# Segment handoff of a recurrent attention kernel: the turned output projection in PSUM, its swap on ScalarE and VectorE, and a new instruction order

## The chip, the cores and the metric

The kernel runs on one core of a Trainium2 chip. The metric is the device time of one launch in microseconds (us). Its engines are TensorE (PE in the profile, its weight loads PEld), VectorE (DVE), ScalarE (ACT), GpSimd (POOL) and SyncE (SP), which issues nearly all DMAs. Matmul results land in PSUM, which here is eight banks of 512 fp32 columns on 128 partitions; everything else that engines read lies in SBUF.

## What is computed

Two attention branches over the same 2048 x 512 input are mixed by a gate. Branch A is a recurrence: 64 segments of 32 tokens, each attending to itself and to 8 memory rows, and the memory of the next segment is the attention's own output at the memory rows. So the segments can't run in parallel. Branch B is an attention over four stretches of 512 tokens with a compressive memory, 32 heads of width 16, and doesn't depend on A.

```python
def _A_ref(x, mem0, Wq, Wk, Wv, Wo, seg_len):        # H=32 heads, Dh=128, M=8
    mem = mem0
    for s in range(n_seg):                           # 64
        xs = x[:, s * seg_len:(s + 1) * seg_len, :]  # 32 tokens
        h = jnp.concatenate([mem, xs], axis=1)
        q, k, v = (jnp.einsum('btd,dhe->bhte', h, W) for W in (Wq, Wk, Wv))
        scores = jnp.einsum('bhqe,bhke->bhqk', q, k) * scale
        p = softmax(where(mask, scores, -1e9))
        o = jnp.einsum('bhqk,bhke->bhqe', p, v)
        o = jnp.einsum('bhte,hed->btd', o, Wo)
        mem = o[:, :M, :]
        outs.append(o[:, M:, :])
...
return g * a + (1 - g) * b                           # g: sigmoid gate, b: branch B
```

## The kernel before

**Recorded operations, one fixed order.** Each piece of work is recorded with `P.op(engine, function, reads, writes, cost, prio)` or `P.dma(...)` (class `Prog`). Where `engine` is a tuple, either engine may do it. The order of the operations on each engine, and with it the choice between such engines, is not decided at build time: it is decoded from a packed string `ORDER` by `sequences()`. `schedule()` replays this order to assign PSUM banks, and `waits()` then derives the semaphore waits from the recorded reads and writes. For a PSUM bank, readers on different engines are put one after the other (`_add`, the loop over `r.readers`); readers on the same engine need no wait.

**One segment** (`p_seg`). From `hT`, the transposed input of the segment (24 of its tokens and the 8 memory rows on the columns, in two buffers used in turn), `project` makes keys, queries and values (matmuls in L1413, copies out of PSUM in L1002). `ktr` transposes keys and queries (L1483), `p_s` makes scores (L1498, L1502) and their exponentials (L1506), `p_u` sums (L1521), logarithm and reciprocal (L1525, L1527) and normalises (L1529, L1531), `f_pv` and `f_pw` multiply with the values (L1562, L1571), and L1002 copies the result into `OT`. Then `wo` makes the output projection.

**The handoff** (`wo` with `mem`). The 64 matmuls of L1310 leave, in 256 columns of one PSUM bank (`so`), four partial results on four groups of 32 partitions: two halves of the heads by two halves of the 512 output columns. The next segment needs the 8 memory rows, transposed and summed over the two halves of the heads, in `hT[1 - par][:, :, 24:32]`. Four steps get them there:

- the turn, L1329: VectorE transposes the 256 columns in 32 x 32 blocks into the tile `rc_sb`;
- two swaps, L1332: 64 partitions each change sides, 32 columns, from `rc_sb` to `rc_sb`, on ScalarE or GpSimd;
- the addition, L1334: VectorE adds the 32 turned and the 32 swapped columns of `rc_sb` into `hT`.

The first projection of the next segment waits for that. Beside it, the segment's own rows leave the same bank: a copy of one half to SBUF (`par`, L1336 by way of L1002, on ScalarE or VectorE) and the row addition L1342 into `ao`, from where a DMA takes them to HBM. After that the bank is free.

**Filler.** Between a segment's dependent steps TensorE does work that doesn't hang on the recurrence: keys, queries and values of the remaining 8 tokens of each segment, four segments at a time (`p_rest`, operand `xr` in L1413; their output projection is `wor`, operand `OTr_sb` in L1310), and all of branch B (L1025 and L1027, L1142 logits with the exponentials of L1160 and the masks of L1166 on GpSimd, L1183, and in `p_bout` the multiplications of L1217 on VectorE or GpSimd). Their places in the order decide how much stands between the last output projection and the first matmul that needs the addition.

Of the kernel before, what the change touches and what calls it, by code (L numbers as in the profile page):

```python
# [7 lines left out]
ACT = mybir.ActivationFunctionType  # L8
ALU = mybir.AluOpType
# [10 lines left out]
    "tQ3F7hsUJr(E}cQ2Vff0LY4_Gapld#8q6^|@KasVT?tP>;{8RK8LP&4Tfpi_POsYA9rJKN2Q|&(>I10Z13d9!aaR93HJpkWlA;jb$Gw6sJ3`6YD?Ogu)r;+d;n!J<UJ3N)V)Vpm&"  # L20
    "H0PIL<K934t1hX4DGSVC&irXItS$5jX2`mq0r8><BGOiHSf|gorw~mPz=UnXH^S(sBC_K1<hj}LjAJ;?4`wVfWm$A7V0P0hr;`{Td>SF^Yy+V~g5fz5B1~}(Yr2(A0hT6ynJz(NS"
    "WiTz$a-Thz{Bc?!6Jy;o|l4G<XXj~fF{>SWD)sHwC^j@Ue<o}I>62$bt37U<0JLSu5Vl%2`u<MDd*A=7*&s&1}ov_DOtX5<wU6T<dtX*i0O7xnQYK~5)Ol41o`W8ND%A^QL}dik("
    "^jFEV?v!UY!yBgP$h>#lVh{Tl)Kq-Y|IAN~pTOG17A!V{*gGBH+)bnm7ucR5Ce9{Pq!{!LpBM9meDUSU`Z3N?V*bAep%37Q#%NYte6}jEwb*e*Cmj)XIR)odv5RQdtt&73qRMjO>"
    "&kZW81Q2^ExT(x=+9vtZ|}<p5zGr^H8M%S(av=$rx>wl54Y*>6fdY;wOMO01k%Z*SLAT@7##k}B4h)vjL!kY+Q|IgB~AP#TMpij&Azg*$cck>$!i2J$n^lC>|%y43<Q<D~k~rFFc"
    "N)%-z9^IMK{LqvOHp}Va5L5tsCg%X^Z(`*hn2xC%MaF{@>IEB3hA@~*uSU@hnSEa?o=7I~(brh170C%Uzp*l1JMsET;$GH56N^82&VWCsm;JZ-!$-Ki4VbS65BIVULK|&DJg>Ir^"
    "5cHaKPMRdQHC%T=vo60pkPG=9%w4*BP=5*N#Q@$Fe?k&wbePC;Lc-F{j3aad|CW+q^K9mbtq|3g&PlV=pGrH~HW#y?^VO!mkPjeYY}`m96)gL>Q~<asoTHK6B~<g=rT(dA7tjzL?"
    "t&d3=gU@yvd(?|;S@*HoSp$^2Z;4|I!RF=Y|bQUAO7ccu*lL=#{N7OS|fC>Pnw=3oZ{~+|G>nRCl*><#O32K4l)6Z;76zhDwF33*kb1NB273xorej@p9&c_4;a0N@Elofcf$*_W#"
    "!9Dy@vA7b`x<@MGlfTfw4&ZvI@Fj3-mZXPDvE0PlI71okKH_TkLBN;p6!3x(sB>B#;&Iy@XJdpRD?1zo9#HuEI$Fx)_sV1t-CTAIVJ@2$>*+yHyAYnUI~J1W`N?ei|pdm-*l@&<F"
    "|EfLWKiaT4v0CcI)=G8^_8`pfD!Gy`~Cr5mxFVMt+%<XQc;P<tdakCa7KWyMT@&qCfACY#A-sZ75q%cz;~<M=2wO7BCtI-GZH@N?&aNK}^_fs^zXSz(dsD}^^!;vUC<y+((>$P&;"
    "g-USb)tZ62rZUK3gXO<HBK>=S$_z86UTmmZMJGo$6(QdNVQT|Zl0qhf+2f>dM*znlIY)8ZUHD7vJ!bh!@+KO$!Ld;~Hq>|ipTyKKN4TJ@c$O=nC+3|#s%@X1r0<<Mz_zgNGRD-in"  # L30
    "tgb9AP@CcV(z5>ybGJH2JpgDR!0Z|n{M=qP;R3*D@}?urne%f(LIdQ0drfrNH=2-u?d}WZNpxS!%KZ#39g!xTj!84*>J2$tC(evyvZ-FpAY6dXir?GAR3%-szBmdF2+EU-G8C2Ty"
    "jrGO%KLJT_Z6gW_h)?VwzBpxcGDn$IH8Xk43MrD$Ytwbptr(s0<@~38{l+BS^9!4jU+Q|fVVlOga217Hpj|uN<N3OH=+Jp*_21U2n_%xIYCwl7P)SLV2I-V<7CzfPW2}RDP)-hk9"
    "1`Z9!$}p@FTohC+oWnq+=Z4PZqC#LsV#XOBJ^)!UabgRgqPW8AGDb-CLRB!k*T$=1C<5Th|RpZUrZafdXH84b1Qp1V3CFE9*N*z%u0LFqJ~VlMiKGKvGphmaJYKNZOM`Ql&Vl4h0"
    "kI{pC`VI(b|gAu1$dCx#O?MVZ1pQu`591$ZlK90u*qcRn3Q7*FgIq?h=oN>f0qbI=YTUe-E4djHMn$#IH0l>Dyw%mrJg$tnrc?CNDQh>6kXhOY#Q%Yh7`I&}_Gd|q{qGG0xVXO*1"
    "}qr)tQkRcT)J&fcTAbl+S5DFAbtmb#EPL53&-YB3`EiT>f&@l(@eTFWe^W5_*d6t5bvEYX@fc_SvzUMG<VpMx7E(<UccQ&UZY6GqSskr3YFjxa8A7fNM_XVzZXW*0i2|)=ARQ;1J"
    "0m)P#ydC1y{|n_W;g08Vi1Pt70r&bD$ed~RKjauAq`=<@PCsxR9ts0a4ukG^4DuhpO}r!wQkFOvt^Z-FB;*!I$9k-n|CV7iZTVURoH~<m5t-AM9z#znB3t@5qFlX)M9_lE5WL!qq"
    "Ll0R3gy4~=+_g+mLaTWAr~D*z>ST_l2O4UMJ~8Z@OPkv>Yc^@$#AxrI0l@JACVQpmt!lkKmejky!PCjX?C-LZ^4S&z{M)G&6rfNQUbBrNV=RA7aF{y2$@Di--N}5B$%l>hNm>=FP"
    "IqgQt*z#s}}b>UQVbgqBDghlKRNGV6OF`rVy7Fe~3{qef7sS6!&>OH+ci+@3g1b#Yoh@MKqEsn6{dXQ~t(mGI?dNMr%f)Z2OCH!tDnK=L)R4Vv3PO5vm;RPRz;iljPVNO|XUX$KU"
    "9E@i&oxwZ@<H=uJ_7DHueI!iR_1N&6#IV)HIRGSCqx5nOt5;;;)YqlnFRuI*(P66D;1%M`YjBKd83!4m{`<yQ!-3E?k=H7#x_hJ>`tv9R^70AkDj;oxj@OVCK}Jq8itMPCHTB7W9"
# [12 lines left out]
    "vA;G<rWgIEC1?3y%W{GrBL_*cK(w2%S9|Px)#^}XiXiN5YxMXz#^ENxCg2~CL4`*7UJrGscXW?z7`hDw^w?dJ7MdHx-owfGb%yl7vy$7^uH$8TKpFBLr{0>7};|6Xpw;v8UQzc5e"
    "fL|?x%{hA}aRWJBNja<hDP`si!;N$z`YD--M7_*?vv~$vLfqGu=)adQ%4jdRX6=jhrK_w)W`;SWoM%)SLq^pbF$zfV<!Pa&v;a4`tv+>UTu#<ak)|c`ZziCPh1J6QhGMTW*}(Kn0"
# [1579 lines left out]
```

## Time and profile before

| | us |
|---|---|
| median of 3 runs | 825.1 |
| lowest and highest of them | 824.47 and 826.17 |
| profiled execution | 826.82 |
| its span on the core | 824.9 |

Busy times are sums of an engine's own instructions in that span. A row of a group of instructions has: line, engine, operation, what it writes and reads with its shape, count; then busy us and the mean ns of one; then the idle time of the engine before them, and what ended it. A row of waits has: who waited, for whom, us in total, how often, and the longest. A row of the timeline has start and duration in us. TensorE's matmuls overlap: the record of one is longer than the step to the next, and two tiles of 32 columns run beside each other. The granted clock of TensorE was 0.999 over the span.

### The profile page before, as it was taken

Reading aid. Unit: us, or ns where it says so; the run is one execution under the profiler, and the core shown is the slowest. Engines: PE = TensorE matmul, PEld = TensorE weight load, DVE = VectorE, ACT = ScalarE, POOL = GpSimd, SP = SyncE. Lnnn points to the kernel's source line nnn. Section 1 sums busy time; section 2 is a strip of 40 time slices with the busy share of each in tenths; the row PEclk is TensorE's granted clock in tenths of the full one; section 3 lists DMA queues with packets and bytes.
Section 4 is the critical chain, followed back from the end, with each engine's and each line's share of the span. In section 5 each row is a group of like instructions: output and inputs, shape, how many; then the busy total and the mean of one; then the engine's idle time right before and its main releaser. Section 6 shows DMA issues by size and latency. Waiting matters only on the chain.

```text
span 824.9 us, 51903 instructions
## 1 busy us (share of the span) xinstructions
PE 795.8 (96%) x23652; PEld 500.9 (61%) x23652; DVE 670.5 (81%) x1510; ACT 561.1 (68%) x1306; POOL 269.8 (33%) x627
## 2 busy tenths in 40 slices
PE   9899899999999999999999999999999999999988
PEld 4346576666566566566666666665765665666655
DVE  4789778888779779788888888888877788878887
ACT  3577666777677776667767677687656757766763
POOL 3552322233332333322433322333423224323441
PEclk9999999999999999999999999999999999999999
DMA  8982202121110211111011111100111010010001
GB/s 331 414 242 57 47 17 37 41 52 26 27 45 22 46 26 38 33 39 39 15 39 46 38 27 42 38 14 19 49 37 32 25 38 8 15 25 21 21 21 37
DMA packets 71697, 45.15 MB, mean 55 GB/s; under 512 B 50046, under 2 KB 69942, under 8 KB 69942
## 3 DMA queue, kind: packets, MB, share of 16 engines
q1 hardware_dynamic: 70422, 40.92, 17.3%
q8 instruction: 185, 3.03, 1.6%
q10 hardware_dynamic: 1056, 0.92, 0.4%
q14 instruction: 34, 0.28, 0.1%
HBM read 30.33 MB, written 8.87 MB: 48 GB/s over the span
## 4 chain that ended last, share of the span: by engine, by line
PE 82%; DVE 7%; ACT 4%; DMA 2%; issue 2%; SPq 1%; POOL 1%; ACTq 0%; POOLq 0%; DVEq 0%
PE pb L1413 46%; PE pb L1310 16%; PE pb L1025 6%; PE pb L1142 3%; PE pb L1562 2%; PE pb L1183 2%; DMA Wv_sb<-in_A_Wv_dram 2%; PE pb L1521 2%; PE pb L1498 2%; DVE hT L1334 1%; PE pb L1027 1%; DVE rc_sb L1329 1%; ACT PTB L1160 1%; PE pb L1571 1%; ACT rc_sb L1527 1%
## 5 line engine op out<-in xcount | busy, mean ns | idle before, releaser
L1002 ACT ACTIVATE st<-pb 128x512 bf16<-128x512 f32 (+2 forms) x301 | 143.6, 498 | 81.5 <-PE pb L1413 75.0
L1160 ACT ACTIVATE PTB<-pb 128x640 bf16<-128x640 f32 x240 | 158.9, 703 | 25.9 <-PE pb L1142 19.0
L1413 PE MATMUL pb<-Wv_sb,hT 128*32 128x512 bf16 x2048 | 155.2, 380 | 0.0
L1413 PE MATMUL pb<-Wq_sb,hT 128*32 128x256 bf16 (+1 forms) x3072 | 138.0, 308 | 1.7 <-DVE hT L1334 1.1
L1413 PE MATMUL pb<-Wk_sb,hT 128*32 128x512 bf16 x2048 | 133.9, 380 | 2.8 <-DVE hT L1334 2.2
L1310 PE MATMUL pb<-Wo_sb,OT_sb 128*32 128x256 bf16 x4096 | 130.5, 273 | 2.1 <-issue 1.4
L1310 PEld LDWEIGHTS pb<-Wo_sb,OT_sb 128*32 128x32 bf16 x4096 | 101.2, 96 | 14.6 <-issue 3.8
L1413 PEld LDWEIGHTS pb<-Wq_sb,hT 128*32 128x32 bf16 x3072 | 81.2, 97 | 47.0 <-DVE hT L1334 6.0
L1483 DVE STREAM_TRANSPOSE QT_sb<-st 128x256 bf16<-128x256 bf16 (+1 forms) x192 | 94.0, 507 | 6.1 <-ACT st L1002 4.7
L1166 POOL TENSOR_SCALAR_AFFINE_SELECT PTB<-PTB 128x512 bf16<-128x512 bf16 x120 | 77.4, 645 | 57.8 <-ACT PTB L1160 49.6
L1483 DVE STREAM_TRANSPOSE KT_sb<-st 128x512 bf16<-128x512 bf16 x128 | 89.2, 699 | 8.7 <-ACT st L1002 6.6
L1531 POOL TENSOR_TENSOR PT_sb<-PT_sb,rc_sb 128x64 bf16<-128x64 bf16 x87 | 32.1, 369 | 165.9 <-ACT rc_sb L1527 164.2
L1002 ACT ACTIVATE OT_sb<-pb 128x320 bf16<-128x320 f32 (+1 forms) x138 | 57.3, 427 | 42.4 <-PE pb L1571 42.0
L1413 PEld LDWEIGHTS pb<-Wk_sb,hT 128*32 128x32 bf16 x2048 | 53.4, 96 | 51.5 <-DVE hT L1334 10.5
L1002 DVE CAST OT_sb<-pb 128x320 bf16<-128x320 f32 (+2 forms) x122 | 57.6, 477 | 23.6 <-PE pb L1571 22.4
L1525 ACT ACTIVATE rc_sb<-pb 128x160 f32<-128x160 f32 x128 | 38.8, 303 | 41.6 <-PE pb L1521 38.4
L1002 DVE CAST V_sb<-pb 128x512 bf16<-128x512 f32 x85 | 57.8, 681 | 6.5 <-PE pb L1413 5.1
L1413 PEld LDWEIGHTS pb<-Wv_sb,hT 128*32 128x32 bf16 x2048 | 48.5, 97 | 18.2 <-ACT st L1002 0.6
L1329 DVE STREAM_TRANSPOSE rc_sb<-pb 128x256 f32<-128x256 f32 x63 | 28.2, 448 | 36.4 <-PE pb L1310 36.2
L1506 ACT ACTIVATE PT_sb<-pb 128x224 bf16<-128x224 f32 x128 | 45.4, 354 | 9.4 <-PE pb L1502 7.3
L1529 DVE TENSOR_TENSOR PT_sb<-PT_sb,rc_sb 128x160 bf16<-128x160 bf16 x128 | 43.1, 337 | 6.8 <-ACT rc_sb L1527 5.2
L1413 PE MATMUL pb<-Wv_sb,xr 128*32 128x512 bf16 x512 | 43.6, 381 | 4.3 <-DMA rest_v<-stg 2.2
(202 smaller groups left out, 1458.9 us busy)
## 6 DMA issues: line engine op xcount, KB each, us to landing
Wv_sb<-in_A_Wv_dram SPq DMA_DIRECT2D x4, 1024.0 KB, 9.6
Wk_sb<-in_A_Wk_dram SPq DMA_DIRECT2D x4, 1024.0 KB, 19.9
Wq_sb<-in_A_Wq_dram SPq DMA_DIRECT2D x4, 1024.0 KB, 26.8
Wo_sb<-in_A_Wo_dram SPq DMA_DIRECT2D x4, 1024.0 KB, 22.2
rest_v<-stg SPq DMA_DIRECT2D x112, 32.0 KB
rem_v<-rest_v SPq DMA_DIRECT2D x28, 128.0 KB, 2.5
a_rows<-ao SPq DMA_DIRECT2D x63, 32.0 KB
stg<-a_rows SPq DMA_DIRECT2D x15, 128.0 KB
```

The lines of the kernel that those rows point to most:

```text
L1002: self.P.op(("act", "dve"), (lambda a: a.activation(dst, src(), ACT.Copy), lambda d: d.tensor_copy(dst, src())), reads=reads, writes=write ...
L1025: ins = pe.matmul(out[32 * c:32 * c + 32], lhsT[:, 32 * c:32 * c + 32], rhs, start=start, stop=stop, tile_position=(0, 32 * c), **kw)
L1160: P.op("act", (lambda dst=dst, src=src: lambda a: a.activation(dst, src(), ACT.Exp, scale=0.25))(), reads=[pair], writes=["%s%d_%d" % (nam ...
L1166: P.op("gp", (lambda pt=pt, ii=ii: (lambda g: g.affine_select(pt, pt, ([[0, len(ii)]] if len(ii) > 1 else []) + [[1, 128]], ALU.is_ge, 0.0 ...
L1310: ins = pe.matmul(pb[so.b][p0:p0 + 32, 0:256], tok(r, g, l), half(h, d, q), start=(r == 0 and g == 0 and l < 2), stop=(r == 1 and g == 3 a ...
L1329: P.op("dve", lambda d: d.transpose(rc[:, 0:256], pb[so.b][:, 0:256]), reads=[so], writes=["rc0", "rc1"], name="turn%s" % name, cost=0.45, ...
L1413: ins = pe.matmul(self.pb[sl.b][32 * g:32 * g + 32, 0:hi - lo], x[:, c, 0:32], cols, start=(c == 0), stop=(c == C - 1), tile_position=(0, ...
L1483: op("dve", (lambda dst=dst, src=src: lambda d: d.transpose(dst, src))(), reads=["st%d%s" % (i, tag)], writes=["%sT%d%s" % (kind, r, tag)] ...
L1506: op("act", lambda a: a.activation(PT[:, r, :], pb[rb.b][:, 0:224], ACT.Exp, scale=SCALE), reads=[rb], writes=["PT%d" % r, "PT%dr" % r], n ...
L1525: op("act", lambda a: a.activation(rc[:, r, :], pb[rb.b][:, 0:160], ACT.Ln), reads=[rb], writes=[rr], name="ln%d_%d" % (s, r), cost=t_act( ...
L1529: op("dve", lambda d: d.tensor_tensor(mine[r], mine[r], by_head(rc[:, r, :]), ALU.mult), reads=[rp, rr], writes=[rp], name="nrm%d_%d" % (s ...
L1531: op(("dve", "gp"), tuple((lambda e: e.tensor_tensor(rest[r], rest[r], late(rc[:, r, :]), ALU.mult)) for _ in range(2)), reads=[rp + "r", rr],
```

## The change

The turn writes into the columns 256 to 511 of the same PSUM bank, which were unused. The swaps read there and write a new small SBUF tile `other_sb`; they may stand on ScalarE or VectorE. The addition takes one operand from PSUM and one from `other_sb`. `rc_sb` has no more part in the handoff. Since the swaps and the addition now read the bank, the copy `par`, recorded after them, comes behind them where it is on another engine. The string `ORDER` is new as a whole, so that other operations have moved and changed engines too.

```diff
 ORDER = (
...
+        self.other = t("other_sb", [128, 4, 8], F32)
...
         if mem:
-            rc = self.rc[:, :, :].rearrange("p r x -> p (r x)")
-            turned = rc[:, 0:256].rearrange("p (c e t) -> p e c t", c=4, e=2)
-            other = rc[:, 256:320].rearrange("p (c z) -> p c z", c=4)[:, :, 0:8]
-            P.op("dve", lambda d: d.transpose(rc[:, 0:256], pb[so.b][:, 0:256]), reads=[so], writes=["rc0", "rc1"], name="turn%s" % name, cost=0.45, prio=prio)
+            rt = P.R("turned%s" % name)
+            turned = lambda: pb[so.b][:, 256:512].rearrange("p (c e t) -> p e c t", c=4, e=2)
+            P.op("dve", lambda d: d.transpose(pb[so.b][:, 256:512], pb[so.b][:, 0:256]), reads=[so], writes=[rt], name="turn%s" % name, cost=0.46, prio=prio)
             for e in range(2):
-                dst, src = other[64 * e:64 * e + 64], turned[64 - 64 * e:128 - 64 * e, 1, :, 24:32]
-                P.op(("act", "gp"), ((lambda a, dst=dst, src=src: a.activation(dst, src, ACT.Copy)), (lambda g, dst=dst, src=src: g.tensor_copy(dst, src))),
-                     reads=["rc0", "rc1"], writes=["rcs%d" % e], name="swap%s_%d" % (name, e), cost=(0.24, 0.24), prio=prio)
-            P.op("dve", lambda d: d.tensor_tensor(mem[0], turned[:, 0, :, 24:32], other, ALU.add),
-                 reads=["rc0", "rc1", "rcs0", "rcs1"], writes=[mem[1]], name="hm%s" % name, cost=0.23, prio=prio)
+                dst, src = self.other[64 * e:64 * e + 64], lambda e=e: turned()[64 - 64 * e:128 - 64 * e, 1, :, 24:32]
+                P.op(("act", "dve"), ((lambda a, dst=dst, src=src: a.activation(dst, src(), ACT.Copy)), (lambda d, dst=dst, src=src: d.tensor_copy(dst, src()))),
+                     reads=[so, rt], writes=["other%d" % e], name="swap%s_%d" % (name, e), cost=(0.24, 0.19), prio=prio)
+            P.op("dve", lambda d: d.tensor_tensor(mem[0], turned()[:, 0, :, 24:32], self.other[:, :, :], ALU.add),
+                 reads=[so, rt, "other0", "other1"], writes=[mem[1]], name="hm%s" % name, cost=0.2, prio=prio)
         self.copy(part[64:128, :], lambda: pb[so.b][64:128, 0:256], 256, [so], rhl, "par%s" % name, prio + 0.2 if mem else prio)
```

More of the change, by code (lines that the diff above doesn't have):

```diff
@@ L20 @@
[L20 to L27, printed above, removed]
@@ new lines @@
+    "zC1H3k$WQ((DM{c2-)s&z1LT+tx@?nS6MVx%YTSKUYlS{=Jp=l{0aUCvGZRcUrdSWn;W`iDj}qfD9MXw>P<+q4U3aSkbS3yOLmu(Thk$G!A;%xUhldx<;kj%@;<xw~e#IL#bFV*z"
+    "ob2+?Lf%=xo)4Dw6PJzjf?cm?q3VUR9OAVPK(mX`f}prB6!=bBVao^a0y8R(*#N^Am6a8Dh0*xF@fNy=QJXv)AfPCZ)7$k+C!rC0Gv)z!IYrxlJvbcTAu$RiGyQMY*<PorPrfw^O"
+    "gezet<E%uH2_VU%9_U~LFoOS2Q7l${{yi+E%mz8>(H#Gmoh8bL09WGb8%PMj<WW>`cYrv$8o`E<avLvff;z)t57=>Jq0*Cb>T!<3hBSf@(lq(0q#AKVyzR<c@{if?OWzNFJ=QXqf"
+    "a8f^;#4M+v=g!LJ7MK@d`dS!g<U|iTU61xCm?+AS+FPWdIY7-Sv?oXEPac5E?c>4~dC=>;f1pd$^*!EdW1e3PzT08};GdVT1*pl)nwT{*aNedUnF=r9@BoQiV2?ZTYuMDMog24qK"
@@ L81 @@
+    "u|;();_7a+m;*n}(S{q1db?`4R-i~H6gLscY$l~ny+;v<=ggwPk7_0oRVN0bmRYoLRt(}EJSB?C1c^FL`*qF7S^zpq$9W_okvnk#ji`Ez0st5?P*5gO&hL7=_Pp11BCc$*#94Eqd"
+    "li@W?0&~ZhaAX5uy!6*&mRgviaNn{sI9ZB&Kf1{E{ur9AJVxSx?b?0P6u-mQPq<)Ct@yrME>6b74%(`kX}%>KSe8G>x!!0pqXD>OArdG?WXE<*4flV^?>Dh)UQ0tbDhblPT%Fjbo"
+    "H5xC>nVxof1*kfe+PDD*d0S8(w-lp-vuhq>*5aNT=K=EK*q=!K6tG=;U+(E<lLj+@=W5EE`azp1NS<+7Y>mRdjFZq&WibV*ivgDYF9sg3CGhAGO()Rf-l6k-B4}qgYE+)E<vG_wk"
+    "ZZ3~!39l<KrdaZKvW7t!n={vRU^a99"
 )
```

113 lines of the change are left out of this document (56 added, 57 removed).

## The prediction

> **What bounds the kernel now.** I read the busy shares and the chain that ended last first, then who waited for whom, then one line at a time, then two handoffs in the timeline.
>
> ```profile
> span 824.9 us, 51903 instructions
> PE 795.8 (96%) x23652; PEld 500.9 (61%) x23652; DVE 670.5 (81%) x1510; ACT 561.1 (68%) x1306; POOL 269.8 (33%) x627
> ...
> PE 82%; DVE 7%; ACT 4%; DMA 2%; issue 2%; SPq 1%; POOL 1%; ACTq 0%; POOLq 0%; DVEq 0%
> PE pb L1413 46%; PE pb L1310 16%; PE pb L1025 6%; PE pb L1142 3%; PE pb L1562 2%; PE pb L1183 2%; DMA Wv_sb<-in_A_Wv_dram 2%; PE pb L1521 2%; PE pb L1498 2%; DVE hT L1334 1%; PE pb L1027 1%; DVE rc_sb L1329 1%; ACT PTB L1160 1%; PE pb L1571 1%; ACT rc_sb L1527 1%
> ```
>
> TensorE is the bound: 96% busy, 82% of the chain. VectorE has 7% of the chain, and two of the lines touched by the change, the addition (L1334) and the turn (L1329), have 1% each. So an edit pays only where TensorE waits for them. The waits of TensorE and of its weight loads say how often:
>
> ```profile
> PE pb L1413 <- DVE hT L1334: 3.2, 10, 0.8
> ...
> PEld pb L1413 <- DVE hT L1334: 16.4, 37, 1.3
> ...
> PEld pb L1413 <- DVE ao L1342: 3.5, 11, 0.5
> ```
>
> The first projection of a segment waits for the addition in 37 of 63 handoffs at the weight loads (16.4 us) and in 10 at the matmuls (3.2 us). Now the groups of instructions in the handoff, by shape:
>
> ```profile
> L1413 PE MATMUL pb<-Wk_sb,hT 128*32 128x512 bf16 x2048 | 133.9, 380 | 2.8 <-DVE hT L1334 2.2
> L1329 DVE STREAM_TRANSPOSE rc_sb<-pb 128x256 f32<-128x256 f32 x63 | 28.2, 448 | 36.4 <-PE pb L1310 36.2
> L1334 DVE TENSOR_TENSOR hT<-rc_sb 128x32 bf16<-128x32 f32 x63 | 20.5, 326 | 18.9 <-POOL rc_sb L1332 15.2 <-ACT rc_sb L1332 2.6 <-ACT st L1002 0.5
> L1332 ACT ACTIVATE rc_sb<-rc_sb 64x32 f32<-64x32 f32 x66 | 15.0, 228 | 33.6 <-DVE rc_sb L1329 32.3
> ```
>
> The addition takes 326 ns in the mean for 32 columns. Its spread, beside that of L1342, an addition with one operand from PSUM, from the views of one line each:
>
> ```profile
> L1334 DVE TENSOR_TENSOR hT<-rc_sb x63: 182/266/752, 59.1 to 808.3; 128x32 bf16<-128x32 f32 x63
> ...
> L1342 DVE TENSOR_TENSOR ao<-pb,st x63: 415/417/417, 60.4 to 808.5; 64x256 bf16<-64x256 f32 x63
> ```
>
> L1334 lies anywhere between 182 and 752 ns; L1342, eight times as long in columns, never moves by more than 2 ns. Why, a late handoff shows; the first lines are the turn, a swap, the addition and the first matmuls that need it, then GpSimd's:
>
> ```profile
> 306.08 0.45 DVE L1329 STREAM_TRANSPOSE rc_sb<-pb 128x256 f32<-128x256 f32 x1 [0.41 <-PE pb L1310]
> 306.57 0.23 ACT L1332 ACTIVATE rc_sb<-rc_sb 64x32 f32<-64x32 f32 x1
> 306.97 0.65 DVE L1334 TENSOR_TENSOR hT<-rc_sb 128x32 bf16<-128x32 f32 x1 [0.44 <-POOL rc_sb L1332]
> 307.07 0.40 PE L1413 MATMUL pb<-Wv_sb,xr 128*32 128x512 bf16 x4
> 307.67 0.40 PE L1413 MATMUL pb<-Wq_sb,hT 128*32 128x512 bf16 x4 [0.20 <-DVE hT L1334]
> ...
> 306.95 0.62 POOL L1217 TENSOR_TENSOR t_sb<-t_sb,rmem 128x256 f32<-128x256 f32 x1
> ```
>
> GpSimd's L1217, all operands in SBUF, began at 306.95 and ended at 307.57; the addition, begun at 306.97, ended just behind it at 307.62. The filler before the projection had run dry. A handoff without this:
>
> ```profile
> 390.19 0.45 DVE L1329 STREAM_TRANSPOSE rc_sb<-pb 128x256 f32<-128x256 f32 x1
> ...
> 390.68 0.43 DVE L1002 COPY st<-pb 64x256 f32<-64x256 f32 x1
> 390.68 0.23 ACT L1332 ACTIVATE rc_sb<-rc_sb 64x32 f32<-64x32 f32 x1 [0.42 <-DVE rc_sb L1329]
> ...
> 391.13 0.19 DVE L1334 TENSOR_TENSOR hT<-rc_sb 128x32 bf16<-128x32 f32 x1
> 391.19 0.39 PE L1413 MATMUL pb<-Wk_sb,xr 128*32 128x512 bf16 x4
> 391.36 0.42 DVE L1342 TENSOR_TENSOR ao<-pb,st 64x256 bf16<-64x256 f32 x1
> 391.38 0.35 PEld L1413 LDWEIGHTS pb<-Wq_sb,hT 128*32 128x32 bf16 x12 [0.29 <-DVE hT L1334]
> 391.41 0.60 PE L1413 MATMUL pb<-Wq_sb,hT 128*32 128x512 bf16 x8
> ```
>
> Here the weight loads "waited" 0.29 us, but filler started at 391.19 and the projection at 391.41, so TensorE lost next to nothing. The step between groups of four such matmuls is 0.21 us (one unhindered stretch of the chain of waits has 16 in 0.86):
>
> ```profile
> 301.67 0.86 PE pb L1413 x16
> ```
>
> **What a handoff loses now.** The 3.2 us of matmul waits are lost for certain. In each of the 37 load waits up to 0.17 us more hides under the matmul's record, which lasts 0.38 us while the next group could follow after 0.21. So the loss lies between 3.2 and 3.2 + 37 x 0.17 = 9.5 us. I take the middle, 6.4; the two handoffs above lost 0.39 (307.67 less 307.07 less 0.21) and about 0.01.
>
> **The change, step by step.** *The turn* (L1329) writes to PSUM instead of SBUF. No VectorE instruction of this trace writes PSUM. Where it reads costs nothing:
>
> ```profile
> L1235 DVE STREAM_TRANSPOSE t_sb<-pb 128x512 f32<-128x512 f32 x24 | 16.8, 702 | 0.3 <-PE pb L1025 0.2
> L1483 DVE STREAM_TRANSPOSE KT_sb<-st 128x512 bf16<-128x512 bf16 x128 | 89.2, 699 | 8.7 <-ACT st L1002 6.6
> ```
>
> 702 ns from PSUM, 699 from SBUF. Below, the fastest L1329 of the 63 could become the rule, 0.40 us; above, reading and writing one bank could take turns, 0.90. I take the nearest row, 0.45.
>
> *The swaps* leave GpSimd. In the built order of the changed kernel 99 of 126 stand on VectorE and 27 on ScalarE: both on VectorE in 40 handoffs, one on each in 19, both on ScalarE in 4. The nearest VectorE row is a 32-column copy from PSUM, 0.15; ScalarE's two PSUM rows give a slope of 51 ns for 64 columns, so 303 less 128 x 0.8 = 0.20 for 32 columns, and at most L1332's 0.23:
>
> ```profile
> L867 DVE COPY hT<-pb x1: 151/151/151, 25.0 to 25.0; 128x32 bf16<-128x32 bf16 x1
> ...
> L1506 ACT ACTIVATE PT_sb<-pb 128x224 bf16<-128x224 f32 x128 | 45.4, 354 | 9.4 <-PE pb L1502 7.3 <-PE pb L1025 0.6
> L1525 ACT ACTIVATE rc_sb<-pb 128x160 f32<-128x160 f32 x128 | 38.8, 303 | 41.6 <-PE pb L1521 38.4 <-PE pb L1025 2.1
> ```
>
> From the turn's end to the addition's start it was 0.44 us (306.53 to 306.97) and 0.49 (390.64 to 391.13), say 0.47. With both swaps on VectorE it becomes 0.05 (as from 390.64 to 390.68) + 0.15 + 0.02 + 0.15 + 0.05 = 0.42. With one on each engine, 0.05 + 0.21 + 0.05 + 0.15 + 0.05 = 0.51, since two engines read one bank one after the other. The mean is 0.45, 0.02 less than now.
>
> *The addition* gets one operand from PSUM and one from SBUF, like L1342. If that frees it from GpSimd, it takes its minimum, 0.18 to 0.19, instead of 0.326: 0.14 less, and most where it was latest. If not, it stays at 0.326.
>
> [...]
>
> Turn to first matmul was 0.45 + 0.47 + 0.33 + 0.05 = 1.30 us and becomes 0.45 + 0.45 + 0.19 + 0.05 = 1.14. *The new order* adds cover besides. Counting the matmuls between the last output projection and the first that needs the addition, at 0.21 us for four of 512 columns, 27 handoffs have one such group more, 33 the same, 3 less: 5.5 us in all, 0.09 a handoff. The mean gain of 0.16 + 0.09 = 0.25 a handoff stands against a mean loss of 6.4 / 37 = 0.17 in those that wait, and the longest lose their own cause. I let 0.4 us of the 6.4 remain: **minus 6.0**.
>
> That filler is taken mainly from between a segment's second sums (L1521) and its values (L1562): 24 segments have less there, 8 more. TensorE hardly waits there:
>
> ```profile
> PE pb L1562 <- DVE PT_sb L1529: 0.5, 1, 0.5
> ...
> PEld pb L1562 <- DVE PT_sb L1529: 5.4, 16, 0.6
> ```
>
> 16 load waits there become, say, 20, each with 0.1 to 0.2 us lost for the four new ones: **plus 0.5**, and all 5.5 us if that cover was just enough everywhere.
>
> *VectorE's queue* gets 99 x 0.15 = 15 us of swaps. It loses 63 x 0.14 = 9 us of stretched additions, and 13 multiplications (L1217) that the order gives to GpSimd, at 0.42 some 5 us; some copies go either way. In the handoff the swaps fill time in which VectorE sat idle (18.9 us before L1334). The copy of half the rows, which stood between turn and addition on VectorE in 19 handoffs, now comes after the addition, as the bank's readers go in order. I charge **nothing**, hidden behind VectorE's idle 19%; without that cover it is the net few us. GpSimd is 33% busy, its lost swaps held nobody else. The DMA queue on SyncE keeps its order throughout.
>
> TensorE's own work is unchanged but for 39 matmuls fewer (whole instead of four-part ones) and 3 more changes of tile shape: nothing.
>
> Sum: 6.0 - 0.5 = 5.5 us. The span goes from 824.9 to 819.4, the profiled execution's 826.8 (1.9 around the span) to 821.3, and the median of the three runs, 825.1, which is 1.7 below the profiled one, to **819.6**.
>
> **The rivals.** *More than the wait goes* (812): the filler now covers every handoff, and the time hidden under matmul records was all real, 9.5, and neighbouring waits in the handoff close up by some 3.5 more. For it: 37 of 63 wait. Against: filler is fixed work, so one handoff's slack is worth nothing elsewhere.
>
> *No gain* (825): the addition is still stretched (GpSimd competes for its one SBUF operand, or for its output), or filler moved away opens 5.5 us elsewhere. For it: VectorE at 81%. Against: L1342 reads one and writes one SBUF tile and is never stretched.
>
> *Turn in one bank* (836, slower): at 0.90 us the chain is 1.59, 0.29 longer than now; less the added cover 0.09 this is 0.20 x 63 = 13 us on top, less 26 handoffs with some 0.1 of slack, 2.6, plus the 0.5: 825.1 + 11. It decides from a turn of about 0.70 us, where 0.25 eats all relief. Nothing in this trace excludes it; against it only that transposes do not feel their source.
>
> *The bank is held longer* (829, slower): the half-row copy now starts behind the addition. In the second handoff above, row addition L1342 would end at 390.64 + 0.45 + 0.19 + 0.43 + 0.42 = 392.13 instead of 391.78, 0.35 later, and the bank is reused only then. The 11 load waits for it grow by 0.35 to 0.4 each, 4 us, and the gain is gone. Against: in the built order the first instruction that waits for the row stands 3.4 us of matmuls behind the last output projection instead of 2.8, more than the delay.
>
> **How the numbers follow.** Forecast 0.50, more 0.10, no gain 0.18, slow turn 0.10, bank 0.12. About 0.2% (1.7 us) is what a measurement can tell from no change. Faster: 0.46 of the forecast, all of "more", 0.02 of "no gain": 0.58. Same: 0.04 + 0.09 = 0.13. Slower: 0.07 + 0.10 + 0.12 = 0.29. The forecast's own range is 815 (9.5 lost now, all regained) to 824 (the certain 3.2, less cover of 2). The range for all, 812 to 830, leaves out the slow turn and little else.
>
> **What would show it.** Right: the addition at 0.18 to 0.20 us without spread, PSUM swaps at 0.15 on VectorE, the turn at 0.45, and load waits of L1413's line for the addition from 16.4 to below 5 us with matmul waits near zero. Wrong: an addition that still reaches 0.6, a turn above 0.6, more waits for the row addition, or a wait of L1562 for L1529 that has grown by what the handoff gave.

## The result, and the profile after

| | before | after |
|---|---|---|
| median of 16 runs each, on one chip, us | 824.94 | 828.71 |
| lowest and highest | 822.73 and 828.45 | 823.14 and 835.02 |
| ratio after/before, 95% interval | | 1.0044 [1.0023, 1.0066] |
| span of the profiled execution, us | 824.9 | 827.8 |

The changed kernel is slower by 0.44%, some 3.7 us. The forecast of 819.6 us had the wrong sign.

From the page of the changed kernel, its span and its busy times:

```profile
span 827.8 us, 51780 instructions
...
PE 798.0 (96%) x23605; PEld 509.8 (62%) x23613; DVE 680.0 (82%) x1606; ACT 555.1 (67%) x1264; POOL 262.0 (32%) x573
```

VectorE has 96 instructions more and is busy 9.5 us longer (670.5 before), GpSimd has 54 fewer. Next the four steps of the handoff, from the views of one line each (count, then duration in ns: least, median, most; first and last start in us; shape):

```profile
L1333 DVE TENSOR_TENSOR hT<-pb,other_sb x63: 151/191/196, 59.8 to 811.0; 128x32 bf16<-128x32 f32 x63
...
L1328 DVE STREAM_TRANSPOSE pb<-pb x63: 417/465/466, 58.8 to 809.4; 128x256 f32<-128x256 f32 x63
...
L1331 DVE COPY other_sb<-pb x99: 183/192/194, 59.3 to 798.8; 64x32 f32<-64x32 f32 x99
L1331 ACT ACTIVATE other_sb<-pb x27: 189/190/195, 75.9 to 810.2; 64x32 f32<-64x32 f32 x27
```

The addition has lost its spread: 182 to 752 ns became 151 to 196. The turn inside one bank costs 463 ns in the mean (page of the changed kernel) where it took 448. A swap takes 0.19 us on either engine, 0.15 had been forecast for VectorE. So turn and addition are what the forecast wanted, and a swap is 0.04 us dearer. Now who waits for whom (us in total, how often, the longest), first in the changed kernel:

```profile
ACT st L1002 <- DVE hT L1333: 15.5, 16, 2.6
...
DVE KT_sb L1482 <- ACT st L1002: 10.5, 24, 1.6
...
PEld pb L1561 <- DVE PT_sb L1528: 6.8, 19, 1.1
...
PEld pb L1497 <- DVE QT_sb L1482: 6.4, 24, 0.6
...
PEld pb L1412 <- DVE ao L1341: 2.2, 7, 0.6
...
PEld pb L1412 <- DVE hT L1333: 1.6, 5, 0.6
...
PE pb L1561 <- DVE PT_sb L1528: 1.4, 3, 1.0
...
PE pb L1497 <- DVE QT_sb L1482: 0.7, 2, 0.4
...
PE pb L1412 <- DVE hT L1333: 0.4, 1, 0.4
```

Then, in the kernel before, the rows that the prediction doesn't show:

```profile
DVE KT_sb L1483 <- ACT st L1002: 6.6, 23, 0.8
...
DVE QT_sb L1483 <- ACT st L1002: 4.7, 16, 1.3
...
PEld pb L1498 <- DVE QT_sb L1483: 4.0, 17, 0.5
...
PEld pb L1498 <- DVE KT_sb L1483: 1.8, 7, 0.5
```

The waits for the addition fell from 16.4 us in 37 load waits and 3.2 us of matmul waits to 1.6 in 5 and 0.4: the change does at the handoff what it was made for. Other rows have grown. The scores (L1497) wait 6.4 us in 24 for the query transposes where it was 4.0 in 17 (L1498 before); the values (L1561) wait 6.8 and 1.4 us for the normalisation, which was 5.4 and 0.5 (L1562 before); VectorE's key transposes wait 10.5 us for ScalarE's copies, 6.6 before. Neighbouring rows fell, so this is not a sum of the loss: the query transposes wait 1.6 us for the copies instead of 4.7, and the values 1.3 us for the second line of the normalisation (L1530) instead of 2.8 (L1531). And ScalarE's half-row copies, which never waited for the addition, now do so for 15.5 us, 16 times.

The last point shows best in one handoff, the one nearest to the second handoff quoted in the prediction, from the timeline of the changed kernel (start, duration):

```profile
391.57 0.47 DVE L1328 STREAM_TRANSPOSE pb<-pb 128x256 f32<-128x256 f32 x1 [1.09 <-PE pb L1310]
392.07 0.41 DVE L1331 COPY other_sb<-pb 64x32 f32<-64x32 f32 x2
...
392.35 0.83 PE L1412 MATMUL pb<-Wk_sb,xr 128*32 128x512 bf16 x12
392.51 0.19 DVE L1333 TENSOR_TENSOR hT<-pb,other_sb 128x32 bf16<-128x32 f32 x1
...
392.74 0.43 DVE L1002 COPY st<-pb 64x256 f32<-64x256 f32 x1
...
393.00 1.04 PE L1412 MATMUL pb<-Wk_sb,hT 128*32 128x512 bf16 x16
...
393.48 0.42 DVE L1341 TENSOR_TENSOR ao<-pb,st 64x256 bf16<-64x256 f32 x1
```

The addition ends at 392.70 and the projection starts at 393.00, with filler up to then, so TensorE doesn't stand still here. But the half-row copy starts 0.70 us after the turn's end (392.04 to 392.74), where it was 0.04 (390.64 to 390.68), and the row addition ends 1.86 us after it (393.90), where it was 1.14 (391.78). Over all 63 handoffs, each matched with its own instructions in both traces, the copy starts 1.02 us after the turn instead of 0.63, and the row addition ends 2.45 us after it instead of 2.12.

### The profile page after: what moved, and what is told of

Read it like the earlier page. It is cut to its first block, busy times and chain, and to the rows that moved or that the text cites. A ratio compares the mean times of both kernels' runs of the same rounds, so it can differ in the third digit from the quotient of the medians.

```text
span 827.8 us, 51780 instructions
## 1 busy us (share of the span) xinstructions
PE 798.0 (96%) x23605; PEld 509.8 (62%) x23613; DVE 680.0 (82%) x1606; ACT 555.1 (67%) x1264; POOL 262.0 (32%) x573
## 4 chain that ended last, share of the span: by engine, by line
PE 80%; DVE 7%; DMA 4%; ACT 3%; issue 2%; POOL 2%; SPq 1%; DVEq 0%; POOLq 0%
PE pb L1412 44%; PE pb L1310 16%; PE pb L1025 6%; PE pb L1142 3%; PE pb L1183 2%; PE pb L1561 2%; PE pb L1497 2%; DMA st<-in_gate_w_dram 2%; PE pb L1520 2%; DMA out_dram<-stg 1%; PE pb L1027 1%; DVE KT_sb L1482 1%; DVE QT_sb L1482 1%; DVE V_sb L1002 1%; PE pb L1570 1%
## 5 line engine op out<-in xcount | busy, mean ns | idle before, releaser
L1412 PE MATMUL pb<-Wv_sb,hT 128*32 128x512 bf16 x2048 | 154.3, 380 | 0.7 <-issue 0.7
L1412 PE MATMUL pb<-Wq_sb,hT 128*32 128x512 bf16 (+1 forms) x3072 | 139.7, 309 | 0.1
L1412 PE MATMUL pb<-Wk_sb,hT 128*32 128x512 bf16 x2048 | 134.4, 380 | 0.6 <-DVE hT L1333 0.4
L1166 POOL TENSOR_SCALAR_AFFINE_SELECT PTB<-PTB 128x512 bf16<-128x512 bf16 x120 | 78.0, 650 | 111.7 <-ACT PTB L1160 105.8
L1412 PEld LDWEIGHTS pb<-Wq_sb,hT 128*32 128x32 bf16 x3072 | 83.4, 97 | 43.3 <-issue 2.4
L1530 POOL TENSOR_TENSOR PT_sb<-PT_sb,rc_sb 128x64 bf16<-128x64 bf16 x81 | 29.1, 359 | 237.5 <-ACT rc_sb L1526 226.4
L1482 DVE STREAM_TRANSPOSE KT_sb<-st 128x512 bf16<-128x512 bf16 x128 | 89.0, 696 | 12.0 <-ACT st L1002 10.5
L1412 PEld LDWEIGHTS pb<-Wk_sb,hT 128*32 128x32 bf16 x2048 | 57.2, 97 | 43.2 <-issue 2.7
L1002 DVE CAST OT_sb<-pb 128x320 bf16<-128x320 f32 (+1 forms) x122 | 57.7, 480 | 20.3 <-PE pb L1570 19.9
L1002 DVE CAST V_sb<-pb 128x512 bf16<-128x512 f32 x89 | 60.5, 680 | 7.4 <-PE pb L1412 6.1
L1412 PEld LDWEIGHTS pb<-Wv_sb,hT 128*32 128x32 bf16 x2048 | 50.4, 97 | 19.7 <-issue 0.6
L1328 DVE STREAM_TRANSPOSE pb<-pb 128x256 f32<-128x256 f32 x63 | 29.2, 463 | 36.0 <-PE pb L1310 35.6
L1002 ACT ACTIVATE stg<-pb 128x512 bf16<-128x512 f32 (+1 forms) x70 | 39.9, 572 | 15.0 <-PE pb L1412 12.1
```

The source lines that it names most:

```text
L1002: self.P.op(("act", "dve"), (lambda a: a.activation(dst, src(), ACT.Copy), lambda d: d.tensor_copy(dst, src())), reads=reads, writes=write ...
L1166: P.op("gp", (lambda pt=pt, ii=ii: (lambda g: g.affine_select(pt, pt, ([[0, len(ii)]] if len(ii) > 1 else []) + [[1, 128]], ALU.is_ge, 0.0 ...
L1328: P.op("dve", lambda d: d.transpose(pb[so.b][:, 256:512], pb[so.b][:, 0:256]), reads=[so], writes=[rt], name="turn%s" % name, cost=0.46, p ...
L1412: ins = pe.matmul(self.pb[sl.b][32 * g:32 * g + 32, 0:hi - lo], x[:, c, 0:32], cols, start=(c == 0), stop=(c == C - 1), tile_position=(0, ...
L1482: op("dve", (lambda dst=dst, src=src: lambda d: d.transpose(dst, src))(), reads=["st%d%s" % (i, tag)], writes=["%sT%d%s" % (kind, r, tag)] ...
L1530: op(("dve", "gp"), tuple((lambda e: e.tensor_tensor(rest[r], rest[r], late(rc[:, r, :]), ALU.mult)) for _ in range(2)), reads=[rp + "r", rr],
```

## The experiments

All kernels compute the whole result. A ratio is the kernel's time over that of the kernel before in runs on the same chip, with its 95% interval. Orders are given as the sequence of the operations of one handoff on an engine: `turn` L1329, `swap` L1332, `hm` the addition L1334, `par` the half-row copy, `row` the row addition L1342 (numbers of the kernel before).

### The two halves of the change: the handoff, and the order

**e1** has the changed code of the handoff in the order of before. **e2** has the code of before in the new order, with the swaps that stood on VectorE put back on ScalarE and GpSimd by planned time, so the new order is not quite as it was made.

```diff
 # e1: changed wo(), order of before, on VectorE:
 turn
-par          (19 handoffs)
+swap_0
+swap_1
 hm
+par
 row
 # e2: wo() of before, new order; swaps off VectorE
```

> The changed handoff (turn in PSUM, swaps, addition from PSUM) in the order of the kernel before: both swaps stand on VectorE right behind the turn, and where the half-row copy stood on VectorE between turn and addition it now stands behind the addition; nothing else is moved. Theory A (the handoff itself gains what was forecast, and the new order loses it elsewhere): the weight loads' wait of L1412 for the addition falls from 16.4 us to under 4, and the time to about 819, 5 to 7 us under the kernel before. Theory B (the handoff code itself costs: VectorE's 126 swaps, ScalarE's half-row copies that wait behind the addition, the bank held longer): the wait falls as well, but the time stays at 825 or goes above, up to 829.

> The handoff of the kernel before (turn into SBUF, swaps on ScalarE and GpSimd) in the order of the changed kernel; the swaps that stood on VectorE are put on ScalarE and GpSimd at the same place of the planned order. Theory A (the new order is what loses): 829 to 835, since the order's losses stay and part of the waits for the addition comes back (6 us less the 5.5 us of added cover). Theory B (the handoff code loses): 825 or less, for the code is the old one and the order is as good as the other.

Measured: e1 1.0042 [1.0025, 1.0059], e2 1.0105 [1.0082, 1.0128]. So each half loses by itself: e1 came out as theory B of its expectation, e2 as theory A of its own. Together they lose no more than e1 alone (1.0044): with the changed handoff the new order neither gains nor costs, with the old one it costs about 1%. Load waits of e1:

```profile
PEld pb L1410 <- DVE ao L1339: 7.1, 20, 0.5
...
PEld pb L1410 <- DVE hT L1331: 5.6, 16, 0.9
...
PEld pb L1495 <- DVE QT_sb L1480: 5.0, 19, 0.8
...
PEld pb L1495 <- DVE KT_sb L1480: 3.0, 7, 0.9
```

In the old order too the waits for the addition shrink, from 16.4 us to 5.6. But the waits for the row addition, which frees the bank, double from 3.5 us in 11 to 7.1 in 20, and those of the scores for the transposes grow from 4.0 and 1.8 to 5.0 and 3.0. The row addition ends 2.27 us after the turn in the mean, 0.15 later than before. The waits of e2:

```profile
DVE KT_sb L1480 <- ACT st L999: 10.5, 27, 1.4
...
PEld pb L1559 <- DVE PT_sb L1526: 7.4, 22, 1.1
...
PEld pb L1495 <- DVE QT_sb L1480: 6.9, 24, 0.7
...
PE pb L1559 <- DVE PT_sb L1526: 1.4, 3, 1.0
```

These are the rows that had grown in the changed kernel (10.5, 6.8, 6.4 and 1.4 us), with the handoff's old code. The row addition ends 2.56 us after the turn here, later than in the changed kernel (2.45). So the grown waits of the last section come with the new order, whichever code the handoff has, and so does the late row addition; the new code alone makes it 0.15 us later.

### Only the stretch taken away

**e11** is the kernel before with one more wait: the GpSimd instruction that follows a swap waits for the addition. Nothing else is changed; the operands stay in SBUF.

```diff
+        for o, after in zip(gp, gp[1:]):       # gp: GpSimd's order
+            if o.name.startswith("swap") and not after.name.startswith("swap"):
+                after.deps.append(by["hm" + o.name[4:].split("_")[0]])
         P.schedule()
```

> The kernel before, handoff, order and engines unchanged, but the GpSimd instruction that follows a swap on GpSimd waits for the addition. If the forecast's mechanism is right (GpSimd's reads of SBUF stretch the addition) the addition falls from 326 ns to about 190 without touching anything else, and the 6 us that the forecast put on it show: ratio 0.992 to 0.997. If the waits for the addition were hidden or are given back at the next step, 0.998 to 1.002.

Measured: 0.9955 [0.9932, 0.9978], and once more beside other kernels (e19, below) 0.9934 [0.9904, 0.9963]: 3.7 and 5.5 us less than the kernel before, and so faster than both kernels. Its addition, by the view of one line, and its load waits:

```profile
L1341 DVE TENSOR_TENSOR hT<-rc_sb x63: 151/193/195, 58.5 to 807.0; 128x32 bf16<-128x32 f32 x63
```

```profile
PEld pb L1420 <- DVE hT L1341: 8.8, 27, 0.8
...
PEld pb L1420 <- DVE ao L1349: 4.0, 12, 0.5
PEld pb L1505 <- DVE QT_sb L1490: 3.9, 17, 0.5
...
PEld pb L1505 <- DVE KT_sb L1490: 1.8, 8, 0.3
...
PE pb L1420 <- DVE hT L1341: 0.5, 2, 0.3
```

With all operands in SBUF the addition takes 151 to 195 ns, as long as GpSimd stands still: it was GpSimd that stretched it. In the kernel before, the addition at 438.83 took 0.66 us beside GpSimd's L1166, which began at 438.81 and took 0.63. With one operand from PSUM no such stretch shows: in the changed kernel the addition at 611.28 took 0.19 us while GpSimd's L1166 ran from 611.20 for 0.64, and none of the 63 took more than 196 ns. What is to be seen in the other rows is that they stay where they were: 4.0, 3.9 and 1.8 us against 3.5, 4.0 and 1.8. So the forecast's gain exists, and the changed kernel gives back nearly twice as much.

### Only the half-row copy moved

**e3** is the kernel before with the 19 copies that stand between turn and addition on VectorE put behind the addition. In **e4**, besides, the copies on ScalarE wait for the addition, as in the changed kernel.

```diff
 turn
-par          (19 handoffs, e3 and e4)
 hm
+par
 # e4
-self.copy(part[64:128, :], ..., 256, [so], rhl, ...)
+self.copy(part[64:128, :], ..., 256, [so] + ([mem[1]] if mem else []), rhl, ...)
```

> The kernel before, with one thing moved: in the 19 handoffs where the copy of half the rows stands on VectorE between turn and addition, it now stands right behind the addition. Theory C (the changed code's loss is this copy, pushed out of VectorE's idle time in the handoff into the busy stretch before the scores): 826 to 829 against 825 (or the same ratio on another chip, 1.002 to 1.005), with a later first key transpose (L1483). Theory D (the copy is hidden; the loss comes from the two swaps on VectorE or from the turned block in PSUM): no change within 0.2%, or a little faster because the addition gets free of the copy.

> The run before this one, and besides the half-row copy waits for the addition on ScalarE too, as the order among the bank's readers forces it to in the changed kernel; handoff and order are the old ones otherwise. Theory C in its wider form (all that the later copy and row addition push back): slower than the run before it, ratio 1.005 to 1.009 to the kernel before, with the load waits of L1413 for the row addition L1342 up from 3.5 us to 6 or more. Theory D: no change to that run.

Measured: e3 1.0024 [0.9999, 1.0048], e4 1.0021 [0.9999, 1.0043]. The move of 19 copies costs some 2 us in the mean although it lets the addition start earlier; the wait of ScalarE's copies adds nothing that can be seen. Both intervals touch 1, so this alone did not settle it.

### On top of e11: small copies, the half-row copy, both

With the stretch gone, each suspected cost of VectorE's queue can be added alone. **e16**: two copies of 64x32 elements into unused columns right behind the turn, in the 44 handoffs that have no half-row copy there; nothing waits for them. **e17**: the move of e3. **e18**: both, the small copies in all 63 handoffs. **e19, e20, e21** are e11, e16 and e17 again, side by side on one chip.

```diff
 # VectorE, on top of e11
 turn
+copy 64x32   (e16: 44 handoffs; e18: 63)
+copy 64x32
-par          (19 handoffs, e17 and e18)
 hm
+par
 row
```

> As e11 (the handoff and order of before, the GpSimd instruction behind a swap waits for the addition; ratio there 0.9955), and besides VectorE does two more copies of 64x32 elements from the turned rows in SBUF into unused columns, right behind the turn, in the 44 of 63 handoffs in which no half-row copy stands there: VectorE gets work like the swaps, nothing waits for it, and the turn stays in SBUF. 'VectorE's time in the handoff costs': the ratio goes up by 0.3 to 0.6 per cent to 0.999 to 1.001, with more load waits of the scores' line for the query and key transposes. 'Hidden behind VectorE's idle time', as the prediction had it: the ratio stays at 0.995 to 0.997.

> As e11, and the 19 half-row copies that stand between turn and addition on VectorE are moved behind the addition (as e3, which cost 0.24 per cent on top of the kernel before). 'The delay of the half row costs': 0.997 to 0.999. 'It costs nothing once the addition is short and early': 0.995 to 0.997.

> As e17, and the two small copies on VectorE behind the turn in all 63 handoffs: VectorE's queue in the handoff is that of e1 (turn, two small copies, addition, half-row copy), but the swaps that count are still on ScalarE and GpSimd and the turn is in SBUF. 'VectorE's queue is the cause': the sum of e16's and e17's costs, 1.001 to 1.004, near e1's 1.0042. 'PSUM and its readers are the cause': 0.995 to 0.998.

> The kernel of e11 once more, beside e20 and e21. Both theories: 0.994 to 0.998.

> The kernel of e16 once more. 'VectorE's added instructions are hidden': within 0.2 per cent of e19. 'They cost': above e19 by 0.3 per cent or more.

> The kernel of e17 once more. 'The half-row copy behind the addition costs': above e19 by 0.2 to 0.5 per cent. 'It is hidden': within 0.15 per cent of e19.

| | first | again, side by side |
|---|---|---|
| e11, e19: stretch gone | 0.9955 [0.9932, 0.9978] | 0.9934 [0.9904, 0.9963] |
| e16, e20: and two small copies | 0.9915 [0.9889, 0.9942] | 0.9956 [0.9928, 0.9984] |
| e17, e21: and half-row copy behind | 0.9986 [0.9964, 1.0008] | 0.9996 [0.9972, 1.0020] |
| e18: and both | 1.0013 [0.9994, 1.0032] | |

The half-row copy behind the addition costs: the mean of its two columns is 0.9991, that is 0.46% or 3.8 us above e11's 0.9945, and in the second column the intervals of e19 and e21 don't meet. Whether the small copies cost isn't settled. The mean of their two columns is 0.9936, as low as e11's, but e16 and e11 ran on different chips. On one chip each, e20 is 0.22% above e19 and e18 0.27% above e17, with intervals that overlap; 0.22% lies between what e20's expectation has for hidden and for costly. Load waits of e16, then of e17:

```profile
PEld pb L1514 <- DVE QT_sb L1499: 3.9, 17, 0.5
PEld pb L1429 <- DVE ao L1358: 3.9, 12, 0.4
...
PEld pb L1514 <- DVE KT_sb L1499: 2.2, 9, 0.5
```

```profile
PEld pb L1418 <- DVE ao L1347: 6.8, 19, 0.6
...
PEld pb L1503 <- DVE QT_sb L1488: 5.2, 20, 0.5
PEld pb L1503 <- DVE KT_sb L1488: 3.3, 12, 0.7
...
PE pb L1503 <- DVE QT_sb L1488: 0.5, 2, 0.3
PE pb L1503 <- DVE KT_sb L1488: 0.5, 1, 0.5
```

In e16 all three rows are nearly e11's. In e17 the bank is freed later (6.8 us of load waits in 19 against 4.0 in 12), and so are the transposes, which stand behind copy and row addition in VectorE's queue (5.2 and 3.3 against 3.9 and 1.8, and 1.0 us of matmul waits). Matched operation by operation and averaged over the 62 segments that follow a handoff, e17's first key transpose starts 2.50 us behind the first projection instead of 2.43, and the last step of the output projection starts 10.255 us behind it instead of 10.189: 0.066 x 62 = 4.1 us in all, near the 3.8 found in the times. The second pair repeats this: 10.252 us in e21 against 10.166 in e19, 5.3 us in all, where the times differ by 5.1.

The 1.0013 of e18 lies between the two theories it was to tell apart, and its interval overlaps e17's. What stands between e18 and e1 (1.0042, the intervals just overlap) isn't settled.

### Moved to ScalarE

Four kernels take work off VectorE again. **e9** is e1 with the 19 half-row copies on ScalarE; **e12** is e1 with both swaps of 62 handoffs on ScalarE; **e14** has both. **e13** is the changed kernel with 39 of its 40 VectorE half-row copies on ScalarE.

```diff
 # e9, e14: par of 19 handoffs; e13: par of 39 handoffs
-VectorE: par
+ScalarE: par
 # e12, e14: both swaps of 62 handoffs
-VectorE: swap_0, swap_1
+ScalarE: swap_0, swap_1
```

> The first experiment (changed handoff, old order) with the 19 half-row copies that stood behind the addition on VectorE put on ScalarE instead, behind the addition there; the turn stays in the bank of the projection. Theory C (the copies cost VectorE's stretch before the scores): the waits of the scores (L1497) for the transposes fall back to the level of the kernel before, ratio 0.996 to 1.001 against the first experiment's 1.004. Theory D (swaps on VectorE): still 1.003 to 1.005.

> The first experiment with both swaps on ScalarE in 62 handoffs, so that VectorE gets no new instruction; the half-row copies stay behind the addition. Theory D: 1.000 or less, because VectorE's 126 swaps are gone. Theory C: 1.003 to 1.006, the copies are still late and the swaps on ScalarE are no faster (0.19 us each) and hold ScalarE.

> The changed handoff in the order of before, with both swaps of 62 handoffs on ScalarE and the 19 half-row copies too that stood between turn and addition on VectorE: VectorE gets no work that it did not have before. 'VectorE's queue pays' (what VectorE was given delays its transposes and normalisations): each of the two edits alone brought 0.3 to 0.4 per cent, so both bring the ratio below the kernel before, 0.996 to 0.999, and the load waits of the scores' line for the key and query transposes fall to the 4.0 us of before. 'ScalarE pays instead': ScalarE has 62 more swaps of 0.19 us and 19 copies that wait for the addition; its late copies hold the transposes back as much as VectorE did, ratio 1.000 to 1.004, with load waits of the scores' line at 5 us or more and more waits of VectorE's key transposes for ScalarE's copies than the 6.6 us of before.

> The changed kernel with 39 of its 40 half-row copies on VectorE put on ScalarE, at the planned time right behind the addition. Theory C: VectorE is rid of 39 x 0.43 = 17 us in the stretch after the handoff, ratio 0.996 to 1.000 against 1.0044. Theory D: 1.003 to 1.006; if ScalarE becomes late, above.

Measured: e9 1.0012 [0.9992, 1.0032], e12 1.0004 [0.9986, 1.0023], e14 1.0038 [1.0015, 1.0061], e13 1.0065 [1.0044, 1.0086]. Either move alone takes most of e1's loss back, both together take back next to nothing, and none of the four is below 1. e9 lies next to the range of theory C, in which the copies cost (up to 1.001), and e12 next to that of theory D, in which the swaps on VectorE do (1.000 or less): so the swaps can't be called free. e14 came out as 'ScalarE pays instead', and e13 even above its range. ScalarE becomes late instead, which e13's waits show:

```profile
DVE KT_sb L1480 <- ACT st L1000: 12.3, 27, 2.3
...
PEld pb L1410 <- DVE ao L1339: 6.3, 12, 0.8
```

The key transposes wait 12.3 us for ScalarE's copies (10.5 in the changed kernel), the bank's next user 6.3 (2.2 there). On either engine the copy starts behind the addition.

### The turn in a bank of its own

**e6** is e1 with the turned columns in another bank in 62 of 63 handoffs, so that swaps and addition no longer read the bank of the half rows. **e8** besides has e9's copies on ScalarE, where they no longer wait for the addition.

```diff
-            rt = P.R("turned%s" % name)
-            turned = lambda: pb[so.b][:, 256:512]
+            rt = P.slot("F")
+            turned = lambda: pb[rt.b][:, 256:512]
```

> The changed handoff in the order of the kernel before (as in the first experiment), but the turn writes into a bank of its own in 62 of 63 handoffs, so that the half-row copy on ScalarE needs not wait for swaps and addition; the 19 copies on VectorE stay behind the addition. Theory C, wider form: most of the first experiment's loss goes, ratio 0.995 to 1.000, and the row addition's waits fall back to some 3.5 us. Theory D: the ratio stays at 1.004, since swaps and turn are the same.

> As the run before, and the 19 copies move to ScalarE, to the place where the old order had a swap there. Theory C: VectorE is rid of 19 x 0.43 = 8 us in the stretch before the scores, and the forecast gain shows, ratio 0.990 to 0.996. Theory D: 1.002 or more. If ScalarE is the one that is late, slower than the run before.

Measured: e6 1.0047 [1.0026, 1.0068], e8 1.0027 [1.0005, 1.0050]. Both are the numbers of theory D, but another cost has come in that neither theory had. The kernel's eight banks are few. Waits of e6's logits of branch B (L1141), which have no such rows before:

```profile
PEld pb L1141 <- DVE hT L1333: 7.0, 5, 1.8
...
PE pb L1141 <- DVE hT L1333: 4.7, 5, 1.3
```

Five times the logits wait for a bank that only the addition sets free, 4.7 us of TensorE standing still. In e8 the scores' load waits for the query transposes are back at the 4.0 us of before, but these bank waits stay (4.9 us): so neither run tells the swaps' cost from the half row's.

### The new order without the stretch

**e15** is e2 with the wait of e11 in 58 handoffs.

> The handoff of before in the changed kernel's order (as in e2, ratio there 1.0105), and besides the GpSimd instruction behind a swap waits for the addition in 58 of the 59 handoffs that have a swap on GpSimd. This takes the stretch of the addition away, as in e11, which gained 0.45 per cent from it in the old order. 'The new order costs by itself': the ratio falls by 0.4 to 0.6 per cent to some 1.005 and stays well above 1, with the one wait for a staging buffer's transfer near 283 us and the waits of scores and values still there. 'The new order is only as bad as the stretch in it': the ratio falls to 0.996 to 1.000, as e11.

Measured: 1.0077 [1.0049, 1.0104], 0.28% below e2 (the intervals overlap), about 1.2% above e11. The new order is dear by itself, with the old handoff at least, in which I placed the swaps; the values wait here for the normalisation for 8.0 us at the loads and 1.6 at the matmuls, as in e2. One piece of it is a transfer that the changed kernel waits for too; the timeline there, at the matmuls:

```profile
283.32 1.90 PE L1412 MATMUL pb<-Wk_sb,xr 128*32 128x512 bf16 x16 [2.45 <-DMA out_dram<-stg]
```

By this view TensorE stands still for 2.45 us until a staging tile has been written out. The kernel before has a wait of nearly this length elsewhere, as its list of waits says:

```profile
PE pb L1413 <- DMA rest_v<-stg: 2.4, 2, 2.2
```

That one is down to 0.8 us after the change, so the wait is hardly a net loss; but the new one is followed by a stretch at half the clock (0.50 for 3.41 us, last section).

## Why the prediction was wrong

*The turn*, 0.45: right, 0.463 in the mean, and "Turn in one bank" (0.90) is out.

*The swaps*, 0.15 on VectorE: 0.19. From the turn's end to the addition's start it was to be 0.45; it is 0.51 (0.49 before, matched over all 63).

*The addition*, 0.326 to 0.19: right, and so was the reason. e11 reaches the same duration by holding GpSimd, with nothing else changed: the median is 193 ns there with both operands in SBUF, 191 in the changed kernel with one in PSUM.

*What a handoff loses*, "minus 6.0": the mechanism is shown and the size nearly right. e11 and e19 gain 3.7 and 5.5 us (0.45% and 0.66%) from the stretch alone, and the waits for the addition in the changed kernel fall further than in e11.

*VectorE's queue*, "I charge **nothing**, hidden behind VectorE's idle 19%": this is the step that failed. The half-row copy that "now comes after the addition" isn't hidden: e17 and e21 charge it with 2.6 and 5.1 us, a mean of 3.8. Together with small copies like the swaps (e18) it is 0.68%, 5.6 us, above e11's mean; whether these copies have a share of their own is open, as said above. From e11's mean to e1 it is 0.97%, some 8 us (on different chips), so the half-row copy is about half of what e1 gives back; what the turn in PSUM and its readers add wasn't isolated. VectorE is idle 19% of the time but not behind the handoff, where copy, row addition and the next segment's transposes stand in one queue, and scores and bank hang on its end.

*"The bank is held longer"* at 829 named the mechanism that e17 and e21 show, but only one end of it: in e17 the load waits for the bank grow by 2.8 us, and the transposes are late as well. That its 4 us are near the measured 3.8 is therefore partly luck. So is its delay: it had the row addition 0.35 later, and the changed kernel shows 0.33, but the code alone makes it 0.15 (e1), the rest comes with the order. The built order was held against it, in which TensorE's next use of the bank stands far enough behind. For the bank that was right: the changed kernel's waits for the row addition are 2.2 us, fewer than before.

*The new order's cover*, "plus 0.5": too little, and the second step that failed. The values' waits for L1529 grew by 1.4 us at the loads and 0.9 at the matmuls (those for L1531 fell by 1.5), the scores' for the query transposes by 2.4 and 0.7, and e2 has the same waits without the new handoff. With the old handoff the order costs 1.05% (e2) or, against e11, about 1.2% (e15). With the new handoff it costs nothing more (1.0042 against 1.0044). Why it is dear in the one case and not in the other wasn't isolated, and in e2 and e15 I placed the swaps.

What the changed kernel itself loses by is therefore open. The late half row is shown in the old order; in the new one it doesn't show at the same place. The first key transpose starts 2.53 us behind the first projection in e1, but 2.44 in the changed kernel and 2.43 before; the next turn starts 10.76 us behind it in e1, 10.60 in the changed kernel and 10.66 before. What has grown there is the time from the addition's end to the first projection, in which TensorE runs filler: 0.35 us in the mean of 62 handoffs, 0.22 in e1 and 0.17 before. So filler moved into the handoff is a candidate, and no run tests it alone.

## What to carry to other kernels

An engine's idle share says nothing on the place where work is added: follow what stands behind the new or the moved instruction in its engine's queue, to the next instruction that TensorE needs, not only to the resource that it holds. Where one PSUM bank has several readers, putting the urgent ones first delays the others, and they have users too: here the move of 19 copies behind the addition cost a mean of 3.8 us. When an instruction is stretched by another engine, look first whether that engine can wait: here one dependency gained 3.7 and 5.5 us, which the new data path could not keep. And where a change comes with a new order, run each half alone: here both lost.

## What the hardware showed besides

*A wait of 2.45 us was followed by half the clock.* Around the wait that ends at 283.32, three stretches of the changed kernel show (start and end, length, busy us and instructions of PE, PEld, DVE, ACT and POOL, granted clock, DMA share, GB/s):

```profile
279.89:283.30 3.41, 0.98 (x36) 0.68 (x28) 1.60 (x6) 1.79 (x3) 0.03 (x1) 0.96 0.32 84
283.30:286.71 3.41, 3.39 (x44) 1.67 (x48) 1.40 (x2) 0.39 (x1) 1.42 (x3) 0.54 0.05 14
286.71:290.13 3.42, 3.42 (x104) 1.92 (x96) 2.25 (x6) 2.07 (x4) 0.00 (x0) 1.00 0.02 5
```

TensorE was busy for 0.98 us of the first, and in the second it got about half its clock (0.54): the 16 matmuls of L1412 at 283.32 took 1.90 us, where 16 such took 0.86 in the stretch quoted in the prediction. At finer edges the clock was 0.50 from 283.06 to 286.47, for 3.41 us, and 1.00 before and behind; in the 3.42 us ahead of it, from 279.64, TensorE was busy for 1.23. Half the clock for 3.41 us is a loss of 1.7, an estimate, on top of a wait of 2.45. Not every wait of about this length goes with it: in the kernel before, TensorE waited 2.23 us for `rest_v` (L1413) until 86.56 and was busy for 1.76 of the 3.41 us from 82.57 to 85.98, and its clock was 1.00 up to 89.40. What makes the difference was not shown. In 147 executions of the kernel before, spread over six chips, the 85 with a mean granted clock of 0.999 or more took 828.2 us in the mean, the 53 at 0.997 or 0.998 (the profiled execution of the changed kernel, with this one stretch, has 0.998) 830.7, and the 9 with a lower one 832.6. So in the mean the 53 are 2.5 us longer than the 85, as much as some of the differences looked for here.

*A VectorE transpose read and wrote one PSUM bank.* 256 columns of fp32 took 463 ns in the mean that way and 448 from PSUM to SBUF.
